# Moving the Nyquist feature of a folded transform from TensorE to the eviction on VectorE

## The chip, the cores and the metric

One core of a Trainium2 chip runs the whole program. In what follows PE is TensorE (matmuls), DVE is VectorE and ACT is ScalarE; PSUM is the memory that matmuls write, and an eviction is the operation that takes a result out of a PSUM buffer and so frees it. The metric is the device time of one execution in microseconds (us). A profile shows one execution; its span is shorter than the time that is reported for the same run (649.2 against 651.07 us for the kernel before).

## The reference

```python
def _attn_ref(x):                      # x: 8 batches x 3008 tokens x 256 features
    X = np.fft.fft(x, axis=1)
    X = np.fft.fft(X, axis=2)
    return X.real.astype(np.float32)

def _moe_ref(x, w_tok1, w_tok2, w_ch1, w_ch2):
    xt = x.transpose(0, 2, 1)
    h = np.maximum(xt @ w_tok1, 0.0) @ w_tok2
    u = x + h.transpose(0, 2, 1)
    h2 = np.maximum(u @ w_ch1, 0.0) @ w_ch2        # d_ch = 1536: most of the arithmetic
    return (u + h2).astype(np.float32)

def reference(**kw):                   # shortened; the mixer is applied to the real part of the transform
    return _moe_ref(_attn_ref(kw["x"]), ...)
```

## The kernel before

The features of a batch are folded into even parts (features 0 to 128) and odd parts (129 to 255) and go through a first product (z). The second-stage product turns them over the feature axis: 12 groups per batch, each with two matmuls into one PSUM buffer `pw`. The first has 259 columns, of which the first 132 exist only for feature 128, the Nyquist term: it enters 130 of them as +0.5 or -0.5 times itself, and the other two are zero. The second has 131 columns and accumulates onto the first.

```python
def ps_mm(name): return psum.tile([P, 512], FP32, tag="mm", name=name, bufs=3)   # first MLP product
def ps_out(name): return psum.tile([P, 512], FP32, tag="o2", name=name, bufs=2)  # second MLP product
def ps_f(name, dt=FP32, n=512):                                                  # all of the transform
    return psum.tile([P, n], dt, tag="f", name=name, bufs=3)

def copy(e, out_, in_):
    if e: (nc.vector, nc.gpsimd)[e - 1].tensor_copy(out=out_, in_=in_)
    else: nc.scalar.activation(out=out_, in_=in_, func=AFT.Copy)

# ... set-up: td1 is 128 x 259; columns 0 to 131 hold only the alternating +-0.5 in row 0 ...

def front(b):                              # a generator: one piece of work per yield
    # ... z ...
    w = perb.tile([P, NG, WD], FP16, tag="w", name="w", bufs=2)
    for g in range(NG):                    # NG = 12 groups, WD = 259
        pw = ps_f("pw")
        za, zb = ...                       # even and odd parts of the group
        nc.tensor.matmul(pw[:, 0:WD], lhsT=zb, rhs=td1[:], start=True, stop=False)
        nc.tensor.matmul(pw[:, 0:131], lhsT=za, rhs=td0[:], start=False, stop=True)
        copy(g % 2 and b == 0, w[:, g, :], pw[:, 0:WD])
        yield
    # ... pt, px, py, pq, pu: the rest of the transform and the token mixing ...
```

The rest of the schedule decides what a longer eviction costs. Batch 0 runs its 12 groups one after another before the MLP begins. The groups of batch 1 are mixed into the MLP of batch 0 in bursts of four per step. The groups of batches 2 to 7 are mixed into the MLP of the batch before, two per step:

```python
plan = [[0] * 11 + [3, 3, 2, 4, 4, 4, 1, 1, 2, 1, 4, 4, 4],        # front(1), during batch 0
        [2] * 4 + [2] * 6 + [1, 1] + [1] * 3 + [1, 2] * 4 + [0]]   # front(b + 1), during batch b > 0
```

A step has six matmuls `pc` of 512 columns, evicted with a relu by ScalarE (two of three) or VectorE (one of three), and twelve matmuls `po` of 256 columns; in every second step VectorE then adds the residual to the output tile `osb`. In the bursts of batch 1 some steps also hold a `pu` product of batch 0, whose VectorE add gives `ut`.

Of the kernel before, what the change touches and what calls it, by code (L numbers as in the profile page):

```python
# [9 lines left out]
FP16 = mybir.dt.float16  # L10
FP32 = mybir.dt.float32
I32 = mybir.dt.int32
AT = mybir.AluOpType
# [6 lines left out]
P = 128  # L20
# [14 lines left out]
WD = 259  # L35
TWO23 = float(2.0 ** 23)
PI2 = float(2 * np.pi)
# [3 lines left out]
def kernel(  # L41
# [9 lines left out]
    nc = tc.nc  # L51
# [8 lines left out]
    const = ctx.enter_context(tc.tile_pool(name="const", bufs=1))  # L60
# [11 lines left out]
    def ps_f(name, dt=FP32, n=512):  # L72
        return psum.tile([P, n], dt, tag="f", name=name, bufs=3)
# [11 lines left out]
    def ts(out_, in_, s1, op0, s2=None, op1=None, eng=nc.vector):  # L85
        if op1 is None:
            eng.tensor_scalar(out=out_, in0=in_, scalar1=s1, scalar2=None, op0=op0)
        else:
            eng.tensor_scalar(out=out_, in0=in_, scalar1=s1, scalar2=s2,
                              op0=op0, op1=op1)  # L90
# [7 lines left out]
                                   in1=pcol[:], op0=AT.mult, op1=AT.add)  # L98
# [7 lines left out]
                                   op0=AT.mult, op1=AT.add)  # L106
# [53 lines left out]
    for t in (tp, tq):  # L160
        for i in range(2):
            h = slice(64 * i, 64 * i + 64)
            nc.scalar.activation(
                out=t[h, :, 64 - 64 * i:128 - 64 * i],
# [15 lines left out]
                                   op0=AT.mult, op1=AT.add)  # L180
# [6 lines left out]
                                   op0=AT.mult, op1=AT.add)  # L187
    nc.vector.scalar_tensor_tensor(out=reff[:], in0=eq32[:], scalar=1472.0, in1=reff[:],
                                   op0=AT.mult, op1=AT.add)
# [3 lines left out]
                                   op0=AT.mult, op1=AT.add)  # L193
    nc.vector.scalar_tensor_tensor(out=offq[:], in0=mid[:], scalar=-752.0, in1=tmp[:],
                                   op0=AT.mult, op1=AT.add)
# [27 lines left out]
    def reduced(m, period, nrow, width, eng=nc.vector):  # L223

        v = gen.tile([P, width], FP32, tag="gv", bufs=2, name="gv")[0:nrow, :]
        eng.tensor_scalar(out=v, in0=m, scalar1=1.0 / period, scalar2=TWO23,
                          op0=AT.mult, op1=AT.add)
        eng.tensor_scalar(out=v, in0=v, scalar1=-TWO23, scalar2=-float(period),
                          op0=AT.add, op1=AT.mult)
        r = gen.tile([P, width], FP32, tag="gr", bufs=2, name="gr")[0:nrow, :]  # L230
        eng.tensor_tensor(out=r, in0=v, in1=m, op=AT.add)
        return r

    def sin(out_, in_, scale):
        nc.scalar.activation(out=out_, in_=in_, func=AFT.Sin, scale=scale)
# [51 lines left out]
    def copy(e, out_, in_):  # L287
        if e:
            (nc.vector, nc.gpsimd)[e - 1].tensor_copy(out=out_, in_=in_)  # L289
        else:  # L290
            nc.scalar.activation(out=out_, in_=in_, func=AFT.Copy)  # L291
# [8 lines left out]
    pl = nc.gpsimd  # L300
# [28 lines left out]
    ts(md[:, 128:255], jrow[:, 1:128], pcol[:], AT.mult, eng=pl)  # L329
    rd = reduced(md[:], 256, P, 255, pl)  # L330
    td0 = const.tile([P, 131], FP16, tag="td0")
    td1 = const.tile([P, WD], FP16, tag="td1")
    sin(td0[:, 2:130], rd[:, 0:128], PI2 / 256)
    sin(td1[:, 132:WD], rd[:, 128:255], PI2 / 256)
    pl.memset(td0[:, 0:1], 1.0)
    ts(td0[:, 1:2], td0[:, 129:130], 0.5, AT.mult, 0.5, AT.add, eng=pl)
    ts(td0[:, 130:131], td0[:, 129:130], 0.5, AT.mult, -0.5, AT.add, eng=pl)
    ts(td0[0:1, :], td0[0:1, :], 0.5, AT.mult, eng=pl)
    pl.memset(td1[:, 0:132], 0.0)
    pl.memset(td1[0:1, 0:2], 0.5)  # L340
    pl.memset(td1[0:1, 3:130:2], 0.5)
    pl.memset(td1[0:1, 2:130:2], -0.5)


    tcol, sgn = pvec("tcol"), pvec("sgn")
# [29 lines left out]
    def w2_cols(b, c):  # L375
        return (w2p if b else w2v)[:, :, :, 8 * c:min(8 * c + 8, NQ)]
# [30 lines left out]
    def front(b):  # L407
# [3 lines left out]
        for t0 in (11, 6, 1):  # L411
            for half in range(2):
                c = slice(half * P, (half + 1) * P)
                pz = ps_f("pz")
                for k in range(5):
                    nc.tensor.matmul(pz[:, 96 * k:96 * k + 96], lhsT=eo[:, t0 + k, c],  # L416
                                     rhs=t1n[:].rearrange("p a b k -> p (a b k)"),
                                     start=True, stop=True)
# [4 lines left out]
        for half in range(2):  # L423
# [3 lines left out]
                             rhs=t1n[0:NQ, half, 0, :],  # L427
                             start=True, stop=True)
            if half:
                nc.tensor.matmul(pz[0:1, 0:24], lhsT=eo[0:NQ, 0, P:P + 1],  # L430
                                 rhs=t1n[0:NQ, 0, 0, :], start=True, stop=True)
            nc.tensor.matmul(pz[:, 24:96], lhsT=eo[:, 16, c],  # L432
                             rhs=t1b[:].rearrange("p a k -> p (a k)"),
                             start=True, stop=True)
# [3 lines left out]
        w = perb.tile([P, NG, WD], FP16, tag="w", name="w", bufs=2)  # L438
        for g in range(NG):
            pw = ps_f("pw")  # L440
            za = z[:, 0, 2 * g:2 * g + 2, :].rearrange("p a b -> p (a b)")
            zb = z[:, 1, 2 * g:2 * g + 2, :].rearrange("p a b -> p (a b)")
            nc.tensor.matmul(pw[:, 0:WD], lhsT=zb, rhs=td1[:], start=True, stop=False)  # L443
            nc.tensor.matmul(pw[:, 0:131], lhsT=za, rhs=td0[:], start=False, stop=True)  # L444
            copy(g % 2 and b == 0, w[:, g, :], pw[:, 0:WD])
            yield


# [1 line left out]
        for th in range(2):  # L450
            c = slice(th * P, (th + 1) * P)
            pt = ps_f("pt1")
            for o, n, f, hw in ((0, 130, 0, hp), (130, 127, 132, hq)):
                for g in range(NG):
                    nc.tensor.matmul(pt[:, o:o + n], lhsT=hw[:, g, c],
                                     rhs=w[:, g, f:f + n],
                                     start=(g == 0), stop=(g == NG - 1))
            if th == 0:
                px = ps_f("px")
                nc.tensor.matmul(px[:, 0:NG], lhsT=perm[:], rhs=w[:, :, 130],  # L460
                                 start=True, stop=True)
# [15 lines left out]
        for c in range(3):  # L477
            py, pq = ps_f("py"), ps_f("pq")
            for o, f, tab in ((pq, 131, tq), (py, 1, tp)):
                for k in range(4):  # L480
                    g = 4 * c + k
                    nc.tensor.matmul(o[:, P * k:P * k + P], lhsT=w[:, g, f:f + P],  # L482
                                     rhs=tab[:, g, :], start=True, stop=True)
            qs = perb.tile([P, CW], FP32, tag="qs", name="qs", bufs=2)
            nc.scalar.activation(out=qs[:], in_=pq[:], func=AFT.Copy)  # L485
            for h, op in ((0, AT.subtract), (1, AT.add)):
                nc.vector.tensor_tensor(out=yt[:, h, CW * c:CW * c + CW], in0=py[:],  # L487
                                        in1=qs[:], op=op)
# [4 lines left out]
        for c in range(NCH):  # L493
            f0 = CW * c
            n = min(CW, S - f0)
            for h in range(2):
                minus = c >= 3
                pu = ps_f("pu")
                for th in range(2):
                    nc.tensor.matmul(pu[:, 0:n], lhsT=uu[:, th, int(minus), h, :],  # L500
                                     rhs=w2_cols(b, c)[:, th],
                                     start=(th == 0), stop=(th == 1))
# [3 lines left out]
                else:  # L506
                    y = yt[:, h, f0:f0 + n]
                nc.vector.tensor_tensor(  # L508
                    out=ut[:, h, f0:f0 + n].rearrange("p (a b) -> p a b", b=64),
                    in0=pu[:, 0:n].rearrange("p (b a) -> p a b", b=64),  # L510
                    in1=y.rearrange("p (a b) -> p a b", b=64), op=AT.add)
# [71 lines left out]
    if BB > 1:  # L583
        x_tiles[1] = load_x(1)
    own = front(0)
    take(own, 4)
    carried(tts_p, hp)
# [17 lines left out]
    for b in range(BB):  # L605
        nxt = front(b + 1) if b + 1 < BB else iter(())
        done, folded = 0, False
        for c in range(NCH):
            c1 = work.tile([P, NCT, CW], FP16, tag="c1", name="c1", bufs=2)
            box = {"rt": turned_u.pop((b, c))}  # L610
            for s in range(4):
                sub = 4 * c + s
                mm1(b, c, c1, range(3 * s, 3 * s + 3))
                if prev is not None:
                    mm2(*prev, s, pbox)
                if b == 0:
                    if s % 2 == 0:
                        take(own, 1)
                    if sub < 8:
                        align_w2(sub)  # L620
                n = plan[b > 0][sub]
                take(nxt, n)
                done += n
                if s == 2 and c + 1 < NCH:
                    turned_u[b, c + 1] = turn_u(b, c + 1)
                if s == 3 and c + 1 == NCH and b + 1 < BB:
                    turned_u[b + 1, 0] = turn_u(b + 1, 0)
                if done >= 8 and not folded:
                    folded = True
                    if b + 2 < BB:  # L630
                        take(fold(b + 2, [nc.gpsimd] * 4), 4)
                    if b + 3 < BB:
                        x_tiles[b + 3] = load_x(b + 3)
            prev, pbox = (b, c, c1), box
# [32 lines left out]
```

## Time and profile before

| | before |
|---|---|
| time, median of 4 runs | 650.1 us (649.53 to 650.5) |
| TensorE (PE) busy | 624.4 us, 96% of the span |
| VectorE (DVE) / ScalarE (ACT) busy | 51% / 49% |
| chain that ended last | 93% PE |

These lines are from the page of the kernel before: the busy times, the chain, and the groups of the second-stage product. A group's columns are line, engine, operation, output<-input, shape and count, then busy time and mean ns of one, then the idle time of its engine before it.

```profile
span 649.2 us, 11895 instructions
PE 624.4 (96%) x4826; PEld 430.7 (66%) x4826; DVE 333.1 (51%) x726; ACT 317.4 (49%) x667; POOL 244.5 (38%) x242
...
PE 93%; DVE 3%; DMA 1%; ACT 1%; issue 1%; DVEq 0%; POOL 0%; POOLq 0%; ACTq 0%
...
L291 ACT ACTIVATE w<-pw 128x259 f16<-128x259 f32 x90 | 30.1, 386 | 50.4 <-PE pw L444 49.9
...
L443 PE MATMUL pw<-td_305,z 128*128 128x259 f16 x96 | 21.4, 274 | 0.9 <-ACT w L291 0.6
L444 PE MATMUL pw<-td_304,z 128*128 128x131 f16 x96 | 18.8, 221 | 0.0
```

PE is the limit. The time that a matmul adds is not the mean duration of its group (274 and 221 ns above), because matmuls overlap; it is the distance from its start to the start of the next. The timeline of the kernel before shows it for one step of batch 2 (columns: start, duration, engine, instruction, count, and the idle time before it):

```profile
139.59 0.27 PE L443 MATMUL pw<-td_305,z 128*128 128x259 f16 x1
139.71 0.22 PE L444 MATMUL pw<-td_304,z 128*128 128x131 f16 x1
139.76 0.27 PE L443 MATMUL pw<-td_305,z 128*128 128x259 f16 x1
139.87 0.22 PE L444 MATMUL pw<-td_304,z 128*128 128x131 f16 x1
...
139.93 1.46 PE L533 MATMUL pc<-ut,wc1p 128*128 128x512 f16 x6
```

Two groups take 139.93 - 139.59 = 0.34 us; a 259-column matmul takes about 0.11 us of it and a 131-column one about 0.057 us. PE never waits here.

Batch 0 is different. The timeline of the kernel before from its first group on:

```profile
31.51 0.27 PE L443 MATMUL pw<-td_305,z 128*128 128x259 f16 x1
...
34.82 0.85 PE L455 MATMUL pt_535<-w,hp 128*128 128x130 f16 x12
...
36.18 0.18 PE L460 MATMUL px<-w,perm 128*128 128x12 f16 x1
...
36.55 0.27 ACT L464 ACTIVATE sq<-pt_535 128x127 f32<-128x127 f32 x1
...
36.85 0.16 DVE L466 COPY uv<-pt_535 128x2 f32<-128x2 f32 x1 [1.57 <-ACT sq L464]
```

Twelve groups would stream in 12 x 0.166 = 2.0 us; they take 3.31 us up to the next product, pt, because three PSUM buffers wait for the evictions: the fourth group starts at 32.32 us, 0.05 us after ScalarE's first eviction has ended (31.88 + 0.39 = 32.27 us). I use the distance from the first pw to px, 36.18 - 31.51 = 4.67 us, as the length of this stage: pt reads the groups of w one after another, so it can begin before the evictions are through (here at 34.82 us, while the last of them ends at 35.27 us), and px comes when they are. The last two lines show something: the VectorE copy to uv needs nothing that ScalarE makes, and still starts only 0.03 us after ScalarE's sq from the same buffer has ended.

In batch 1, the timeline of the kernel before shows the third group of the first burst waiting for a buffer (two lines of other engines are put in):

```profile
87.04 0.27 PE L443 MATMUL pw<-td_305,z 128*128 128x259 f16 x1
...
87.24 0.69 DVE L508 TENSOR_TENSOR ut<-pu,yt 128x512 f16<-128x512 f32 x1 [1.14 <-PE pu L500]
...
87.41 1.47 ACT L291 ACTIVATE w<-pw 128x259 f16<-128x259 f32 x4 [1.72 <-PE pw L444]
87.84 0.27 PE L443 MATMUL pw<-td_305,z 128*128 128x259 f16 x1 [0.31 <-ACT w L291]
...
88.18 1.46 PE L533 MATMUL pc<-ut,wc1m 128*128 128x512 f16 x6
```

The third group starts 0.04 us after ScalarE's first eviction of the burst has ended (87.41 + 0.39 = 87.80 us), and 0.09 us before VectorE's add to ut ends (87.24 + 0.69 = 87.93 us). So it waited for ScalarE, as the trace says, and not for the buffer of the pu product just before the burst.

### The profile page before, as it was taken

Reading aid. Unit: us, or ns where it says so; the run is one execution under the profiler, and the core shown is the slowest. Engines: PE = TensorE matmul, PEld = TensorE weight load, DVE = VectorE, ACT = ScalarE, POOL = GpSimd, SP = SyncE. Lnnn points to the kernel's source line nnn. Section 1 sums busy time; section 2 is a strip of 40 time slices with the busy share of each in tenths; the row PEclk is TensorE's granted clock in tenths of the full one; section 3 lists DMA queues with packets and bytes.
Section 4 is the critical chain, followed back from the end, with each engine's and each line's share of the span. In section 5 each row is a group of like instructions: output and inputs, shape, how many; then the busy total and the mean of one; then the engine's idle time right before and its main releaser. Section 6 shows DMA issues by size and latency. Waiting matters only on the chain.

```text
span 649.2 us, 11895 instructions
## 1 busy us (share of the span) xinstructions
PE 624.4 (96%) x4826; PEld 430.7 (66%) x4826; DVE 333.1 (51%) x726; ACT 317.4 (49%) x667; POOL 244.5 (38%) x242
## 2 busy tenths in 40 slices
PE   3789999999999999999999999999999999999996
PEld 3545667577666776667766676666766677666674
DVE  8755436733664346633565336643566336654442
ACT  7547564365535554365534645356533655334431
POOL 8819859659400872029420693009400000000000
PEclk9779999999999999999999999999999999999999
DMA  9992572822822258152852339123221622322332
GB/s 146 179 210 51 93 144 42 148 62 59 165 57 66 61 100 132 34 102 58 128 79 73 61 70 168 41 67 85 59 50 37 106 51 49 81 65 64 81 82 61
DMA packets 86486, 56.27 MB, mean 87 GB/s; under 512 B 54768, under 2 KB 83376, under 8 KB 85680
## 3 DMA queue, kind: packets, MB, share of 16 engines
q1 hardware_dynamic: 78176, 38.04, 27.7%
q0 software_dynamic: 8256, 17.49, 17.0%
q8 instruction: 37, 0.61, 0.4%
q14 instruction: 17, 0.14, 0.1%
HBM read 34.98 MB, written 24.64 MB: 92 GB/s over the span
## 4 chain that ended last, share of the span: by engine, by line
PE 93%; DVE 3%; DMA 1%; ACT 1%; issue 1%; DVEq 0%; POOL 0%; POOLq 0%; ACTq 0%
PE po L552 39%; PE pc L533 38%; PE pu L500 6%; PE pw L443 2%; PE pz L416 1%; DMA xm<-in_x_dram,ix_76 1%; PE pw L444 1%; PE py L482 1%; PE pq L482 1%; PE ph L363 1%; PE ph L365 1%; DVE xp L395 0%; DVE xd L394 0%; DVE yt L487 0%; DVE ut L508 0%
## 5 line engine op out<-in xcount | busy, mean ns | idle before, releaser
L533 PE MATMUL pc<-ut,wc1p 128*128 128x512 f16 x576 | 141.4, 381 | 0.5 <-DVE ut L508 0.4
L533 PE MATMUL pc<-ut,wc1m 128*128 128x512 f16 (+1 forms) x576 | 134.9, 370 | 0.0
L566 DVE TENSOR_TENSOR osb<-po,rt 128x254 f32<-128x254 f32 (+6 forms) x264 | 77.2, 345 | 58.9 <-PE po L552 55.9
L533 PEld LDWEIGHTS <-wc1m 128*128 128x128 f16 x576 | 54.8, 98 | 54.0
L399 POOL TENSOR_TENSOR eo<-xp 94x512 f16<-94x512 f16 (+1 forms) x28 | 33.9, 1211 | 142.8 <-PE pz L432 141.6
L533 PEld LDWEIGHTS <-wc1p 128*128 128x128 f16 x576 | 53.1, 98 | 51.8 <-issue 5.6
L394 POOL TENSOR_TENSOR xd<-xp,xm 94x1024 f16<-94x1024 f16 x28 | 59.3, 2120 | 63.4 <-DMA xm<-in_x_dram,ix_76 63.4
L508 DVE TENSOR_TENSOR ut<-pu,yt 128x512 f16<-128x512 f32 (+1 forms) x96 | 61.4, 669 | 35.6 <-PE pu L500 35.6
L395 POOL TENSOR_TENSOR xp<-xp,xm 94x1024 f16<-94x1024 f16 x28 | 59.4, 2120 | 2.2
L291 ACT ACTIVATE w<-pw 128x259 f16<-128x259 f32 x90 | 30.1, 386 | 50.4 <-PE pw L444 49.9
L291 ACT ACTIVATE z<-pz 128x480 f16<-128x480 f32 (+1 forms) x59 | 34.3, 661 | 28.6 <-PE pz L416 19.5
L500 PE MATMUL pu<-w2p,uu 128*128 128x512 f16 (+1 forms) x168 | 45.0, 379 | 0.4 <-DVE ut L508 0.4
L487 DVE TENSOR_TENSOR yt<-py,qs 128x512 f16<-128x512 f32 x48 | 30.6, 685 | 19.4 <-ACT qs L485 11.5
L403 POOL TENSOR_TENSOR eo<-xd 94x508 f16<-94x508 f16 (+1 forms) x28 | 33.7, 1202 | 0.0
L500 PEld LDWEIGHTS <-uu 128*128 128x128 f16 x192 | 19.0, 99 | 11.6 <-issue 2.6
L485 ACT ACTIVATE qs<-pq 128x512 f32<-128x512 f32 x24 | 14.1, 595 | 19.5 <-PE pq L482 8.7
L443 PE MATMUL pw<-td_305,z 128*128 128x259 f16 x96 | 21.4, 274 | 0.9 <-ACT w L291 0.6
L444 PE MATMUL pw<-td_304,z 128*128 128x131 f16 x96 | 18.8, 221 | 0.0
L474 ACT ACTIVATE uu<-uv 128x256 f16<-128x256 f32 (+2 forms) x48 | 13.2, 337 | 9.9 <-DVE uv L469 9.9
L128 POOL DMA_DIRECT2D xp<-in_x_dram x32 | 17.2, 560 | 0.2 <-issue 0.2
L118 POOL DMA_INDIRECT xm<-in_x_dram,ix_76 x16 | 15.3, 955 | 5.0 <-issue 4.3
L416 PE MATMUL pz<-t1n,eo 94*128 94x96 f16 x240 | 14.4, 208 | 2.7 <-DVE z L289 2.3
(420 smaller groups left out, 1123.1 us busy)
## 6 DMA issues: line engine op xcount, KB each, us to landing
out_dram<-osb SPq DMA_DIRECT2D x88, 256.0 KB, 3.3
xp<-in_x_dram POOLq DMA_DIRECT2D x16, 272.0 KB
xp<-in_x_dram POOLq DMA_DIRECT2D x16, 127.5 KB
rt<-ut SPq DMA_TRANSPOSE x96, 3.2
out_dram<-osb SPq DMA_DIRECT2D x8, 192.0 KB, 3.2
w2s<-in_moe_w_tok_dram POOLq DMA_DIRECT2D x1, 1504.0 KB
w1p<-in_moe_w_tok_dram POOLq DMA_DIRECT2D x2, 384.0 KB
wc_148<-in_moe_w_ch_dram POOLq DMA_DIRECT2D x1, 768.0 KB
```

Of the source, the lines that this page charges most:

```text
L291: nc.scalar.activation(out=out_, in_=in_, func=AFT.Copy)
L394: eng.tensor_tensor(out=xd[:, t, :], in0=xp[:, t, :], in1=rv, op=AT.subtract)
L395: eng.tensor_tensor(out=xp[:, t, :], in0=xp[:, t, :], in1=rv, op=AT.add)
L399: eng.tensor_tensor(out=eo[:, t, 1:129], in0=xp[:, t, 1:129], in1=xp[:, t, 255:127:-1], op=AT.add)
L403: eng.tensor_tensor(out=eo[:, t, 129:256], in0=xd[:, t, 1:128], in1=xd[:, t, 255:128:-1], op=AT.subtract)
L443: nc.tensor.matmul(pw[:, 0:WD], lhsT=zb, rhs=td1[:], start=True, stop=False)
L487: nc.vector.tensor_tensor(out=yt[:, h, CW * c:CW * c + CW], in0=py[:], in1=qs[:], op=op)
L500: nc.tensor.matmul(pu[:, 0:n], lhsT=uu[:, th, int(minus), h, :], rhs=w2_cols(b, c)[:, th], start=(th == 0), stop=(th == 1))
L508: nc.vector.tensor_tensor(out=ut[:, h, f0:f0 + n].rearrange("p (a b) -> p a b", b=64), in0=pu[:, 0:n].rearrange("p (b a) -> p a b", b=64), ...
L533: nc.tensor.matmul(pc[:, 0:n], lhsT=wc[:, h, ct * P:(ct + 1) * P], rhs=ut[:, h, f0:f0 + n], start=(h == 0), stop=(h == 1))
L552: nc.tensor.matmul(po[0:n, o:o + D], lhsT=c1[:, ct, ks * P:ks * P + n], rhs=wc2[:, ct, :], start=(ct == 0), stop=(ct == NCT - 1))
L566: nc.vector.tensor_tensor(out=osb[r, ks_, j], in0=src[r, k0:k1, j], in1=rt[r, ks_, p], op=AT.add)
```

## The change

Feature 128 leaves the first product, which shrinks from 259 to 128 columns: one for the share of feature 128 and 127 for the rest. The second product no longer accumulates. At the eviction ScalarE copies the 127 columns, and VectorE computes `alternating row x share + the other 131 columns` in one instruction, taking the share as a column of per-partition scalars from the same PSUM buffer.

```diff
-    td1 = const.tile([P, WD], FP16, tag="td1")
+    td1 = const.tile([P, P], FP16, tag="td1")
+    alt = const.tile([P, 131], FP16, tag="alt")
...
-    pl.memset(td1[:, 0:132], 0.0)
-    pl.memset(td1[0:1, 0:2], 0.5)
-    pl.memset(td1[0:1, 3:130:2], 0.5)
-    pl.memset(td1[0:1, 2:130:2], -0.5)
+    pl.memset(td1[:, 0:1], 0.0)
+    pl.memset(td1[0:1, 0:1], 0.5)
+    pl.memset(alt[:], 1.0)
+    pl.memset(alt[:, 2:129:2], -1.0)
+    pl.memset(alt[:, 130:131], 0.0)
...
-            nc.tensor.matmul(pw[:, 0:WD], lhsT=zb, rhs=td1[:], start=True, stop=False)
-            nc.tensor.matmul(pw[:, 0:131], lhsT=za, rhs=td0[:], start=False, stop=True)
-            copy(g % 2 and b == 0, w[:, g, :], pw[:, 0:WD])
+            nc.tensor.matmul(pw[:, 131:WD], lhsT=zb, rhs=td1[:], start=True, stop=True)
+            nc.tensor.matmul(pw[:, 0:131], lhsT=za, rhs=td0[:], start=True, stop=True)
+            copy(0, w[:, g, 132:WD], pw[:, 132:WD])
+            nc.vector.scalar_tensor_tensor(
+                out=w[:, g, 0:131], in0=alt[:], scalar=pw[:, 131:132],
+                in1=pw[:, 0:131], op0=AT.mult, op1=AT.add)
```

More of the change, by code (lines that the diff above doesn't have):

```diff
@@ L331 @@
     td0 = const.tile([P, 131], FP16, tag="td0")
-    td1 = const.tile([P, WD], FP16, tag="td1")
+    td1 = const.tile([P, P], FP16, tag="td1")
+    alt = const.tile([P, 131], FP16, tag="alt")
     sin(td0[:, 2:130], rd[:, 0:128], PI2 / 256)
-    sin(td1[:, 132:WD], rd[:, 128:255], PI2 / 256)
+    sin(td1[:, 1:P], rd[:, 128:255], PI2 / 256)
     pl.memset(td0[:, 0:1], 1.0)
```

## The prediction

> **What bounds the kernel.** TensorE. The page gives PE 624.4 us busy of 649.2 us (96%), VectorE 51%, ScalarE 49%. The chain of waits that ended last is 93% PE, 77% in the two MLP products (po 38.9%, pc 37.8%); the second-stage product (pw) is 2.5%. After 60 us PE's waits on other engines sum to about 1.4 us. A column less to stream is time saved, unless the new eviction makes PE wait.
>
> **What PE saves.** 96 products of 259 columns become 128 columns. In the timeline, the next product follows a 259-column one after 0.110 us and a 131-column one after 0.057 us; runs of 130/127-column products, each with its own weight load, go at 0.055 us each. So 128 columns should cost 0.056 us: 0.054 us saved per group, 96 x 0.054 = 5.2 us at most.
>
> **What is added and moved.** The eviction was one instruction: ScalarE 128x259, 386 ns (90), or a VectorE copy, 426 ns (6, first batch). It becomes a ScalarE copy of 127 columns (sq, same shape: 0.27 us) and a VectorE operation on 131. Its like is the 128x127 add from PSUM to uv: 0.28 us, the next 0.20 us after. VectorE gets about 96 x 0.28 = 27 us more, less 2.5: 55% busy. ScalarE loses about 9 us.
>
> The two engines will not read the bank at once. [...]the 2-column copy pt to uv, which needs nothing from ScalarE, starts 0.03 us after ScalarE's sq from the same bank ends. So a pw buffer is held by ScalarE, then by VectorE: about 0.6 us, not 0.39, plus whatever VectorE is at. There are three such buffers.
>
> **On the critical path.**
> - Batches 2 to 7 (72 groups): two groups per step of about 2.9 us. Even behind 0.75 us of output adds the buffers are free before the next step. Full gain: 72 x 0.054 = 3.9 us.
> - Batch 1 (12 groups, 87 to 96 us, bursts of four): the fourth group waits for the first one's buffer, now behind VectorE's ut add (0.62 to 0.69 us) or osb adds (0.75 us). Estimated net loss 0.1 to 0.4 us per burst, 0.7 us in all.
> - Batch 0 (12 groups in a row, 31.5 to 34.8 us, paced by evictions that alternated between two engines): every group now needs both in turn. About 1.0 us from product to free buffer, over three buffers: 4 us against 3.1. Net loss about 0.8 us.
> - Set-up on GpSimd: one small memset more, off the path.
>
> Sum: -3.9 + 0.7 + 0.8 = -2.4 us: 648.0 us, within 2%. Range 645.2 to 650.8. Chances: faster by over 2% 0.01, within 2% 0.97, slower by over 2% 0.02.
>
> **What would show it.** By group: pw's first product at about 218 ns where 274 stood; VectorE's new operation 0.26 to 0.33 us; ScalarE's w copy 0.27 to 0.28. In the timeline: pw pairs 0.11 us long, not 0.166, in batches 2 to 7, without PE waits; the fourth group of a burst in batch 1, and batch 0 from its fourth group on, waiting for VectorE; VectorE's operation beginning just after ScalarE's copy ends.
>
> **What would make it wrong.** If both evictions overlap, batches 0 and 1 lose less: near 645.5. If the scalar read from PSUM makes the VectorE operation 0.6 us long, batch 0 loses 3 us. If VectorE delays pc relus, PE waits appear in the MLP. If weight loads pace the 128-column product, the gain shrinks.

"Bank" stands there for the PSUM buffer that both engines read.

## The result, and the profile after

The changed kernel took 648.91 us (median of 4 runs, 647.04 to 649.84) against 650.1 us before: ratio 0.9979, 95% interval 0.9955 to 1.0003. The prediction was 648.0 us, within 2%. That is the same by the 2% rule, and the interval reaches past 1; that the change saves anything at all is shown by the stages below and by e11_again, not by this result.

The page of the changed kernel, the lines that answer to those above:

```profile
span 646.9 us, 11992 instructions
PE 620.1 (96%) x4826; PEld 427.0 (66%) x4826; DVE 358.4 (55%) x816; ACT 311.4 (48%) x673; POOL 244.8 (38%) x243
...
PE 92%; DVE 3%; POOL 2%; ACT 1%; issue 1%; DVEq 0%; POOLq 0%
...
L291 ACT ACTIVATE w<-pw 128x127 f16<-128x127 f32 x96 | 21.9, 276 | 49.7 <-PE pw L447 49.7
...
L449 DVE SCALAR_TENSOR_TENSOR w<-alt,pw 128x131 f16<-128x131 f16 x96 | 29.5, 352 | 19.3 <-ACT w L291 18.5
...
L446 PE MATMUL pw<-td_305,z 128*128 128x128 f16 x96 | 16.6, 220 | 3.0 <-DVE w L449 1.9 <-DVE ut L514 1.0
```

The product is narrower, ScalarE's copy shorter, VectorE has 29.5 us of new work, and PE now idles 3.0 us before pw where it idled 0.9 us.

The timeline of the changed kernel for a step of batch 2:

```profile
141.23 0.22 PE L446 MATMUL pw<-td_305,z 128*128 128x128 f16 x1
141.29 0.22 PE L447 MATMUL pw<-td_304,z 128*128 128x131 f16 x1
...
141.46 1.46 PE L539 MATMUL pc<-ut,wc1p 128*128 128x512 f16 x6
141.55 0.44 ACT L291 ACTIVATE w<-pw 128x127 f16<-128x127 f32 x2 [1.15 <-PE pw L447]
141.86 0.62 DVE L449 SCALAR_TENSOR_TENSOR w<-alt,pw 128x131 f16<-128x131 f16 x2 [0.99 <-ACT w L291]
```

Two groups now take 0.23 us instead of 0.34 us, without a wait. VectorE begins, at 141.86 us, when ScalarE's first copy is through (141.55 + 0.28 = 141.83 us).

Batch 0 in the timeline of the changed kernel:

```profile
30.81 0.22 PE L446 MATMUL pw<-td_305,z 128*128 128x128 f16 x1
...
31.62 3.98 DVE L449 SCALAR_TENSOR_TENSOR w<-alt,pw 128x131 f16<-128x131 f16 x12
...
32.02 0.22 PE L446 MATMUL pw<-td_305,z 128*128 128x128 f16 x1 [0.70 <-DVE w L449]
...
33.05 0.22 PE L446 MATMUL pw<-td_305,z 128*128 128x128 f16 x1 [0.22 <-DVE w L449]
...
35.12 0.85 PE L461 MATMUL pt_549<-w,hp 128*128 128x130 f16 x12 [0.22 <-DVE w L449]
...
36.48 0.18 PE L466 MATMUL px<-w,perm 128*128 128x12 f16 x1
```

From the first pw to px: 36.48 - 30.81 = 5.67 us, 1.00 us more than before. The fourth group waits 0.70 us for VectorE, and three groups later (33.05 us) the next wait for VectorE follows. So each of the three buffers is held for 33.05 - 32.02 = 1.03 us.

In the first two bursts of batch 1, the timeline of the changed kernel has these waits:

```profile
88.17 0.69 DVE L514 TENSOR_TENSOR ut<-pu,yt 128x512 f16<-128x512 f32 x1 [1.14 <-PE pu L506]
...
88.78 0.61 DVE L449 SCALAR_TENSOR_TENSOR w<-alt,pw 128x131 f16<-128x131 f16 x2
88.91 0.22 PE L446 MATMUL pw<-td_305,z 128*128 128x128 f16 x1 [0.55 <-DVE ut L514]
...
89.18 0.22 PE L446 MATMUL pw<-td_305,z 128*128 128x128 f16 x1
...
92.10 0.76 DVE L572 TENSOR_TENSOR osb<-po,rt 128x258 f32<-128x258 f32 x2 [0.62 <-PE po L558]
...
92.77 1.38 DVE L449 SCALAR_TENSOR_TENSOR w<-alt,pw 128x131 f16<-128x131 f16 x4
...
93.17 0.22 PE L446 MATMUL pw<-td_305,z 128*128 128x128 f16 x1 [0.77 <-DVE w L449]
```

In the first burst the third group waits 0.55 us for the ut add, which ends at 88.17 + 0.69 = 88.86 us, and the fourth starts 0.05 us after VectorE's first operation on w has ended (88.78 + 0.35 = 89.13 us). In the second burst VectorE is adding residuals to osb until it can turn to w, so the fourth group waits 0.77 us. From its first pw to the next pc, the three bursts take 1.32, 1.38 and 1.26 us where they took 1.14, 0.98 and 1.14 us.

To compare stages and not whole times, I read three lengths from the timeline of each profile: batch 0 from its first pw to px; batch 1 from its first pw to its first pt; and the mean distance between the first pt of one batch and that of the next for batches 2 to 7.

| kernel | batch 0, us | batch 1, us | one of batches 2 to 7, us |
|---|---|---|---|
| before | 4.67 | 11.54 | 75.18 |
| changed | 5.67 | 12.25 | 74.54 |
| difference | +1.00 | +0.71 | -0.65 each, -3.9 for six |

The three differences sum to -2.2 us, and the two profiled executions differ by -2.3 us. The sum is not a proof by itself: the part before the first group of batch 1 also moves from run to run, as told below. In these two profiles the first pw of batch 0 came 0.70 us earlier in the changed kernel, and the stretch from px to batch 1 lasted 0.63 us longer, so the two nearly cancel. Nor is this pair a fair sample of whole times: the profiled execution of the kernel before took 651.07 us, more than any of its four timed runs.

### The profile page after: what moved, and what is told of

Read it like the earlier page. It is cut to its first block, busy times and chain, and to the rows that moved or that the text cites. A ratio compares the mean times of both kernels' runs of the same rounds, so it can differ in the third digit from the quotient of the medians.

```text
span 646.9 us, 11992 instructions
## 1 busy us (share of the span) xinstructions
PE 620.1 (96%) x4826; PEld 427.0 (66%) x4826; DVE 358.4 (55%) x816; ACT 311.4 (48%) x673; POOL 244.8 (38%) x243
## 4 chain that ended last, share of the span: by engine, by line
PE 92%; DVE 3%; POOL 2%; ACT 1%; issue 1%; DVEq 0%; POOLq 0%
PE po L558 39%; PE pc L539 38%; PE pu L506 6%; PE pz L419 1%; PE pw L446 1%; PE pw L447 1%; PE py L488 1%; PE pq L488 1%; DVE ut L514 1%; DVE yt L493 0%; DVE osb L572 0%; PE ph L366 0%; PE pz L435 0%; PE ph L368 0%; POOL xm L118 0%
## 5 line engine op out<-in xcount | busy, mean ns | idle before, releaser
L291 ACT ACTIVATE w<-pw 128x127 f16<-128x127 f32 x96 | 21.9, 276 | 49.7 <-PE pw L447 49.7
L449 DVE SCALAR_TENSOR_TENSOR w<-alt,pw 128x131 f16<-128x131 f16 x96 | 29.5, 352 | 19.3 <-ACT w L291 18.5
L446 PE MATMUL pw<-td_305,z 128*128 128x128 f16 x96 | 16.6, 220 | 3.0 <-DVE w L449 1.9
```

The costliest lines, as they stand in the source:

```text
L449: nc.vector.scalar_tensor_tensor(out=w[:, g, 0:131], in0=alt[:], scalar=pw[:, 131:132], in1=pw[:, 0:131], op0=AT.mult, op1=AT.add)
```

## The experiments

Kernels are compared only within the same rounds. "Correct" means that the result agreed with the reference. The stage lengths of the experiments are gathered here:

| run | batch 0, us | batch 1, us | batches 2 to 7, us |
|---|---|---|---|
| e1_late | 4.68 | 11.54 | 74.53 |
| e2_early | 5.67 | 12.25 | 75.18 |
| e3_narrow | 4.69 | 11.20 | 74.54 |
| e4_evict | 5.83 | 12.41 | 75.18 |
| e8_one | 6.47 | 12.65 | 74.54 |
| e9_bufs | 4.87 | 12.25 | 74.54 |
| e10_best | 3.68 | 11.55 | 74.53 |
| e11_again | 5.67 | 12.25 | 74.54 |
| e12_late_again | 4.67 | 11.54 | 74.53 |

The batch 0 stage of e6_banks, which has the change unaltered there, took 6.84 us and not 5.67, because the pt products, from the first to px, lasted 2.54 us instead of 1.36. Its groups took as long as in the change: 4.30 us from the first pw to the first pt, against 4.31. I put it down to a low granted clock, because matmuls also took twice as long where the clock is known: in the profile of before, six pc matmuls from 44.71 us on took 2.89 us at a granted clock of 0.50, against 1.46 us from 139.93 us on at 1.00. In the profiles of before and of the change the granted clock was 1.00 during the stage of batch 0. So I compare a stage only where its matmuls go at the same pace.

My theory: the narrow product saves its columns wherever the buffers come free in time, and the two-step eviction loses time where they do not, in batches 0 and 1. The rivals: the saving per group is just smaller than the columns say, or the difference is noise.

### e1_late: the change in batches 2 to 7 only

```diff
-            (the changed product and eviction)
+            if b >= 2: (the changed product and eviction)
+            else:      (product of 259 columns and single eviction, as before)
```

> The change in batches 2 to 7 only; batches 0 and 1 keep the product of 259 columns and the one eviction. Theory (narrow product saves 0.054 us per group where the buffers are free in time, the two-step eviction costs about 1.0 us in batch 0 and 0.7 us in batch 1): the whole saving stays and the loss goes: 72 x 0.054 = 3.9 us less than before, about 646.2 us, ratio 0.994, and about 1.7 us less than the changed kernel. In the trace batch 0's pw stage is 3.3 us long as before, and each of batches 2 to 7 is 0.65 us shorter. Rival (the saving per group is simply smaller than the columns say, spread over all batches, and nothing is lost at the start): three quarters of the changed kernel's gain, about -1.0 us, ratio 0.9985.

Correct; 647.08 us against 650.73, ratio 0.9946 (0.9928 to 0.9963). The loss in batches 0 and 1 is gone, the gain in the others is whole. The rival's 0.9985 lies outside the interval.

### e2_early: the change in batches 0 and 1 only

```diff
-            (the changed product and eviction)
+            if b < 2: (the changed product and eviction)
+            else:     (product of 259 columns and single eviction, as before)
```

> The change in batches 0 and 1 only. Theory: slower than before by about 1.7 us (ratio 1.0026): batch 0's pw stage 4.3 us instead of 3.3, each burst of batch 1 longer by 0.2 to 0.5 us, batches 2 to 7 as before. Rival (no loss at the start): -0.3 to -1.3 us, ratio 0.998 to 0.9995.

Correct; 652.71 us, ratio 1.0035 (1.002 to 1.005). In these two batches the change costs time, and the stages repeat those of the changed kernel: 5.67 and 12.25 us. With e1_late this places gain and loss.

### e3_narrow: the narrow product alone

```diff
-            copy(0, w[:, g, 132:WD], pw[:, 132:WD])
-            nc.vector.scalar_tensor_tensor(...)
+            copy(g % 2 and b == 0, w[:, g, :], pw[:, 0:WD])
```

> Wrong result on purpose: the product of 128 columns, but the old single eviction of 259 columns and no VectorE operation, in all batches. Shows what the narrow product alone is worth. Theory: 0.054 us per group in batches 2 to 7 and about 0.15 us per burst in batch 1, nothing in batch 0, whose pace is set by the evictions: about -4.3 us, ratio 0.9934. Rival (the weight load paces the 128-column product): under half of that, -2 us or less, ratio 0.997.

Wrong (feature 128 is missing); 646.5 us, ratio 0.993 (0.9914 to 0.9947). Batch 0 is as long as before, batch 1 is 0.34 us shorter, and the other batches are 0.65 us shorter each: 0.65 / 12 = 0.054 us per group. So the weight load did not pace the narrow product here.

### e4_evict: the new eviction alone

```diff
-            nc.tensor.matmul(pw[:, 131:WD], lhsT=zb, rhs=td1[:], start=True, stop=True)
-            nc.tensor.matmul(pw[:, 0:131], lhsT=za, rhs=td0[:], start=True, stop=True)
+            nc.tensor.matmul(pw[:, 0:WD], lhsT=zb, rhs=tdw[:], start=True, stop=False)
+            nc.tensor.matmul(pw[:, 0:131], lhsT=za, rhs=td0[:], start=False, stop=True)
+            # tdw as before; alt set to zero, so the VectorE operation adds nothing
```

> Right result: the product of 259 columns as before, but the new two-step eviction in all batches, with the alternating row set to zero so that VectorE adds nothing. Shows what the eviction alone costs. Theory: +1.0 us in batch 0, +0.7 to +1.0 us in batch 1, nothing in batches 2 to 7: about +1.8 us, ratio 1.0028. Rival (the later evictions also hold up the MLP's own evictions): +3 us or more, with PE waits on pc or po in batches 2 to 7.

Correct; 652.99 us, ratio 1.0037 (1.0021 to 1.0053). Batch 0 is 1.16 us longer than before (a little more than the 1.0 us expected), batch 1 0.87 us, the others exactly as long as before, 75.18 us. So 72 more VectorE operations in the MLP cost nothing that these stages show. The rival of +3 us or more fails.

### e5_forms: which part of the VectorE operation costs what

```diff
+            b == 3: scalar=pcol[:] (SBUF)    b == 4: scalar=0.5
+            b == 5: in0=alt32[:] (fp32)      b == 6, 7: tensor_tensor add of the row, fp16 or fp32
```

> Wrong result on purpose, a look only. The VectorE operation took 0.352 us where 0.26 to 0.33 us were predicted; which part of it costs that? Batches 0 to 2: as in the change (scalar column read from the PSUM bank). Batch 3: scalar from a column in SBUF. Batch 4: a constant. Batch 5: scalar from PSUM, alternating row in fp32. Batch 6: plain add of the fp16 row and the bank, no scalar. Batch 7: plain add with an fp32 row. If the scalar column in PSUM is the cost: batches 3, 4, 6, 7 at 0.28 to 0.29 us, 0, 1, 2 and 5 at 0.35. If the three-operand operation is: 3 and 4 stay at 0.35, only 6 and 7 fall to 0.29. If the fp16 row is: 5 and 7 fall, the others stay.

Its output is wrong, which doesn't matter for the time. The groups of the operation's forms, in the order batches 0 to 2, 5, 3, 7, 4, 6:

```profile
L465 DVE SCALAR_TENSOR_TENSOR w<-alt,pw 128x131 f16<-128x131 f16 x36 | 11.0, 353 | 3.9 <-ACT w L291 3.1
L457 DVE SCALAR_TENSOR_TENSOR w<-alt,pw 128x131 f16<-128x131 f32 x12 | 3.7, 352 | 3.1 <-ACT w L291 3.1
L453 DVE SCALAR_TENSOR_TENSOR w<-alt,pcol,pw 128x131 f16<-128x131 f16 x12 | 3.6, 347 | 3.1 <-ACT w L291 3.1
L462 DVE TENSOR_TENSOR w<-pw,alt 128x131 f16<-128x131 f32 x12 | 2.9, 287 | 3.1 <-ACT w L291 3.1
L455 DVE SCALAR_TENSOR_TENSOR w<-alt,pw 128x131 f16<-128x131 f16 x12 | 2.9, 285 | 3.1 <-ACT w L291 3.1
L459 DVE TENSOR_TENSOR w<-alt,pw 128x131 f16<-128x131 f16 x12 | 2.9, 285 | 3.1 <-ACT w L291 3.1
```

None of my three alternatives fits as I wrote it. With a constant the three-operand operation costs 285 ns, the same as a plain add. A column of scalars adds 62 ns from SBUF and 68 ns from PSUM. So it is the per-partition scalar column that costs, nearly alike from either memory, and neither the third operand nor the fp16 row. It also delays the next operation. The timeline of this run, a step of batch 4 (constant):

```profile
291.42 0.49 DVE L455 SCALAR_TENSOR_TENSOR w<-alt,pw 128x131 f16<-128x131 f16 x2 [0.98 <-ACT w L291]
```

The second operation follows the first after 0.49 - 0.285 = 0.20 us with a constant; with the column in PSUM, in the step of batch 2 shown for the changed kernel, it follows after 0.62 - 0.352 = 0.27 us.

### e6_banks: why VectorE waits for ScalarE

```diff
+            b >= 5: second product into a buffer of its own (pv); scalar from SBUF, in1=pv[:, 0:131]
+            b in (3, 4): one buffer, scalar from SBUF
```

> Wrong result on purpose, a look only. Why does VectorE begin only after ScalarE's copy ends? Batches 0 to 2 as in the change; batches 3 and 4 with the scalar from SBUF, both products still in one bank; batches 5 to 7 the same with the second product in another buffer, so that the two engines read different banks. All write the same output tile. If sharing the bank is the reason: in batches 3 and 4 VectorE still begins after ScalarE's copy of the same group has ended, in 5 to 7 it begins before that end. If the shared output tile or VectorE's own queue is: no difference between 3 and 4 and 5 to 7. (With two buffers per group the products may wait for buffers in 5 to 7; that is not what is looked at.)

Wrong; 655.28 us, because the extra buffers make the products wait (not what is looked at). It was run at another time. First a step of batch 3 (one buffer), then a step of batch 5 (two buffers), from the timeline of this run:

```profile
215.02 0.44 ACT L291 ACTIVATE w<-pw 128x127 f16<-128x127 f32 x2 [1.14 <-PE pw L456]
215.33 0.61 DVE L458 SCALAR_TENSOR_TENSOR w<-alt,pcol,pw 128x131 f16<-128x131 f16 x2 [0.99 <-ACT w L291]
...
370.52 0.45 ACT L291 ACTIVATE w<-pw 128x127 f16<-128x127 f32 x2 [1.14 <-PE pw L448]
370.58 0.35 DVE L451 SCALAR_TENSOR_TENSOR w<-alt,pcol,pv 128x131 f16<-128x131 f16 x1 [0.73 <-PE pv L449]
```

With one buffer VectorE starts 0.31 us after ScalarE, released by it. With two it starts 0.06 us after ScalarE, released by PE, while ScalarE is still copying; the output tile w is the same. So the shared buffer is the reason. Whether it is the memory behind the buffer or the program's own unit of bookkeeping, this run cannot tell.

### e8_one: one VectorE operation for all 259 columns

```diff
-            copy(0, w[:, g, 132:WD], pw[:, 132:WD])
             nc.vector.scalar_tensor_tensor(
-                out=w[:, g, 0:131], in0=alt[:], ..., in1=pw[:, 0:131], ...)
+                out=w[:, g, :], in0=alt[:], ..., in1=pw[:, 0:WD], ...)     # alt zero from column 130 on
```

> Right result, a look only: the eviction is one VectorE operation of 259 columns (alternating row zero beyond column 130), ScalarE takes no part. Theory (what costs in batch 1 is the wait for VectorE's earlier work plus the hand-over; what costs in batch 0 is the hold over three buffers): [...]batch 0's stage is then paced by VectorE alone and longer, 4.8 to 5.1 us against 4.3; batch 1's stretch from its first product to the next stage about as in the change, 12.2 to 12.3 us; batches 2 to 7 at 74.54 us as in the change. Rival (the hand-over is all of the loss): batch 0 at 3.3 to 3.6 us, batch 1 at 11.5.

Correct; 650.68 us. It was run at another time. The operation takes 486 ns, 134 ns more than with 131 columns; twelve in a row lasted 4.88 us in batch 0, so (4.88 - 0.486) / 11 = 0.40 us from one to the next. Batch 0 is 6.47 us to px; to the first pt it is 4.94 us, within what was expected (4.8 to 5.1). Batch 1 took 12.65 us where 12.2 to 12.3 were expected: a miss. Without a hand-over the loss does not shrink, it grows. The rival, that the hand-over is all of the loss, falls. How much the hand-over costs is not measured here, because VectorE's own operation also became longer (486 ns against 352).

### e9_bufs: six buffers in batch 0

```diff
-            pw = ps_f("pw")
+            pw = ps_mm("pw") if b == 0 and g % 2 else ps_f("pw")
```

> Right result: the change, but in batch 0 every second group's product goes to one of the three buffers of the first MLP product, which are free at that time, so six buffers in place of three. Theory (three buffers held about 1 us each set the pace in batch 0): VectorE's operations run back to back at 0.265 us and the stage shrinks from 4.3 us to 3.4 to 3.7; all else as in the change, so about -2.9 us against before, ratio 0.9955. Rival (the hand-over between the engines sets the pace, not the number of buffers): the stage stays at 4.2 to 4.3 us, ratio 0.9965.

Correct; 647.67 us against 650.34, ratio 0.9966 (0.9951 to 0.998). The ratio lies near the rival's number, but the stages decide. From the first pw to the first pt batch 0 took 2.81 us, less than the 3.4 to 3.7 I expected, because pt now starts early and waits for w in its midst. To px it took 4.87 us instead of 5.67. The 12 VectorE operations ran back to back in 3.28 us, or (3.28 - 0.352) / 11 = 0.266 us each. So with three buffers, it was the buffers that set the pace of the new form in batch 0. The stage is still 0.20 us longer than that of the kernel before, which has three buffers; what six buffers do for the old form is shown by e10_best.

### e10_best, e11_again, e12_late_again

The first is e1_late with the six buffers of e9_bufs in batch 0; the second is the change unaltered; the third is e1_late again. They ran together.

> Right result, a try at a version that beats both: the change in batches 2 to 7 only, the old form in batches 0 and 1, and in batch 0 six buffers for the products instead of three. Expected: batch 0 from its first pw product to the product px 0.2 to 0.4 us shorter than the 4.67 us of before; batch 1 as before (11.54 us from its first pw product to the next stage); batches 2 to 7 at 74.54 us: 3.9 + 0.3 = 4.2 us less than before, ratio 0.9935. If buffers are no limit for the old form, as the change in batches 2 to 7 alone: ratio 0.994.

> The change itself, unaltered, timed again beside the two others on one chip, since its first four runs left an interval that touches 1. From the trace's stages (+1.0, +0.7, -3.9): 2.2 us less than before, ratio 0.9966, interval within 0.995 to 0.9985.

> The change in batches 2 to 7 only, again: 3.9 us less than before, ratio 0.994, and 1.7 us less than the change itself beside it.

| run | median, us (before: 650.37) | ratio | 95% interval |
|---|---|---|---|
| e10_best | 645.52 | 0.9929 | 0.9907 to 0.995 |
| e11_again | 648.76 | 0.9984 | 0.9969 to 0.9999 |
| e12_late_again | 645.88 | 0.9942 | 0.9926 to 0.9957 |

All correct. e10_best beats both kernels: its batch 0 is 1.0 us shorter than before, more than the 0.2 to 0.4 us I expected. With six buffers the two engines' evictions run side by side, six groups each; in e9_bufs VectorE has a part in all twelve. The timelines of e10_best, then of e9_bufs:

```profile
32.07 2.17 ACT L291 ACTIVATE w<-pw 128x259 f16<-128x259 f32 x6
...
32.51 2.08 DVE L289 CAST w<-pw 128x259 f16<-128x259 f32 x6
...
31.64 3.28 DVE L449 SCALAR_TENSOR_TENSOR w<-alt,pw 128x131 f16<-128x131 f16 x12
```

So the buffers are not all of the loss in batch 0. Both forms gain from six buffers (the old one 4.67 - 3.68 = 0.99 us, the new one 5.67 - 4.87 = 0.80 us), and with six the new form is still 4.87 - 3.68 = 1.19 us longer than the old one. That VectorE's twelve operations in a row set this rest is read from the lines; no run isolates it. VectorE's plain copies of 259 columns follow each other after (2.08 - 0.415) / 5 = 0.33 us in e10_best, where its operation with a scalar column needed 0.40 us for as many (e8_one).

The advantage of e10_best over e12_late_again in whole time is inside the noise; its batch 0 is clearly shorter. e12_late_again confirms e1_late. e11_again excludes "no gain" only just, and the -2.2 us of the stages (ratio 0.9966) lies just outside its interval, which begins at 0.9969: see the next section. Its ratio is also within the range I expected, but at the far end.

## Why the prediction was right or wrong

The time was predicted within 0.9 us, and most of the reasons held up; two sizes were off, and in batch 1 part of the path. The total by itself proves little: the range given, 645.2 to 650.8 us, also holds the 650.1 us of the kernel before, and the whole times show 1.0 to 1.6 us saved, not 2.4. The stages carry the argument.

**What bounds the kernel: right.** PE is 96% busy before and after, and the chain is 93% and 92% PE.

**The saving per group: right.** Predicted 0.054 us per group and 3.9 us for batches 2 to 7. Measured 0.65 us per batch, 3.9 us for six, with the eviction or without it (the change, e3_narrow).

**VectorE's extra work in the MLP is free: right.** e4_evict leaves batches 2 to 7 at 75.18 us to the hundredth. VectorE went to 55% busy, as predicted.

**Serial eviction because of the shared buffer: right.** In e6_banks VectorE starts 0.31 us after ScalarE with one buffer and 0.06 us after it with two; what it is about the shared buffer that makes VectorE wait was not shown.

**Batch 0 and batch 1: right in kind, batch 0 a little too small.** Predicted net losses of 0.8 and 0.7 us; measured 1.00 and 0.71 us. The predicted hold of about 1.0 us per buffer is what the trace shows (1.03 us for every three groups). That the buffers set the pace of the new form is shown by e9_bufs: six of them take 0.80 us away. They are not the whole cause, because the old form gains as much from six, and then the new form is 1.19 us behind it (e9_bufs, e10_best). In batch 1, e3_narrow (0.34 us shorter) and e4_evict (0.87 us longer) show that the eviction costs the time. The sum was right, but by a partly different path: the fourth group waits behind the osb adds in the second burst, as predicted (0.77 us), while in the first and the third it is the third group that waits longest, for the ut add (0.55 and 0.49 us). That the queue of VectorE work is the cause stands in the timeline; it was not isolated by a run.

**The VectorE operation: mis-sized.** I predicted 0.26 to 0.33 us and took an add without a scalar column as its like; it took 0.352 us, and the next followed after 0.27 us and not 0.20. The missing term is the column of scalars, 62 to 68 ns (e5_forms).

**What stays open: about 1 us between stages and clock on the wall.** The stages say -2.2 us. Whole times say about -1.2 us (650.1 to 648.91) and -1.6 us by the medians of e11_again; the two ratios, 0.9979 and 0.9984, amount to -1.4 and -1.0 us of 650. For e2_early and e4_evict, which also have the new eviction in batch 0, the stages say +1.7 and +2.0 us and the medians +2.0 and +2.3 us. The part of the run that is not in my three stages is the start, up to batch 1. It varies: the first pw of batch 1 came between 85.5 and 89.4 us in the profiles.

One cause is visible. PE's granted clock between 37 and 47 us, where PE waits a good deal, was 0.70 in the profile of before, 0.79 in that of the change and 1.00 in that of e9_bufs (PE busy 7.14, 6.80 and 6.06 us of the 10). From px to the first group of batch 1 it took 49.6 to 49.9 us in four of the thirteen profiles (e2_early, e6_banks, e9_bufs, e12_late_again) and 50.7 to 51.8 us in the nine others. In the profile of before the granted clock was 0.50 from about 41 to 47.5 us, in that of the change from about 43 to 49.5 us. As a mean from 37 to 60 us it was 0.85 in six of the nine (before, after, e1_late, e4_evict, e10_best, e11_again), against 0.93 in e12_late_again and 1.00 in e2_early and e9_bufs; for the other four I have no such figure. What brings the low clock on was not shown. The 33 timed runs of the kernel before show its size: 25 had a mean granted clock of 0.989 or 0.990 and a median of 650.6 us, 8 had 0.994 to 0.997 and a median of 649.0 us. Whether longer waits in batch 0 make the low clock more frequent is not settled; it would take many more profiles.

## What to carry to other kernels

Columns taken from a matmul were worth their streaming time here (0.054 us per group) only where the eviction still freed the PSUM buffer before it was wanted: every one of 72 groups in the steady part paid, and the 24 groups at the start gave back 1.7 us of the 3.9 us. Where two engines evict one buffer in turn, as here (0.28 us by ScalarE, then 0.35 us by VectorE), count it as held for the sum of both, plus what the second engine has in its queue: in batch 0 each buffer was held for 1.03 us. Give such a stretch more buffers or keep the old form there (here the old form with six buffers was the shortest, 3.68 us). Before more buffers are taken for the cure, try them on the old form too. When the expected effect is smaller than the run-to-run spread, measure stages between fixed points of the trace: the six or more timed runs of one kernel in a group spread over 1.2 to 3.5 us, while the stage lengths of equal code repeated within 0.02 us, except for the one stage whose pt products lasted 2.54 us instead of 1.36 (e6_banks).
